# Attention and mixture of experts in one kernel: expert 0's first weights fetched later, and the slots' one-hot matmuls gathered at one place of a unit

## The chip, the cores and the metric

The kernel runs on one core of a Trainium2 chip. The metric is the device time of one execution in microseconds (us); each figure for a kernel is the median of its runs. The engines are TensorE (PE, with its weight loads PEld), VectorE (DVE), ScalarE (ACT), GpSimd (POOL) and SyncE (SP), which here only starts DMA transfers. Each engine works through its own queue in program order.

## The reference

Windowed causal attention, then a layer of 8 experts of which each token uses two:

```python
# q, k, v: [8 batches, 8 heads, 576, 64]; window 64
scores = scale * np.matmul(q, k.transpose(0, 1, 3, 2))
mask = (rel >= 0) & (rel < window)
scores = np.where(mask, scores, -1000000000.0)
...
return np.matmul(attn, v).astype(np.float32)

x = np.ascontiguousarray(attn_out.transpose(0, 2, 1, 3)).reshape(B * S, H * D)   # [4608, 512]
logits = x @ w_gate
noise_scale = np.log1p(np.exp(x @ w_noise))
noisy_logits = logits + noise_scale * noise
top2 = np.argpartition(-noisy_logits, 2, axis=1)[:, :2]
...
for e in range(E):                       # E = 8, w1[e]: [512, 1024], w2[e]: [1024, 512]
    for k in range(2):
        mask = top2[:, k] == e
        h = np.maximum(x[mask] @ w1[e], 0.0)
        out[mask] += top2_w[mask, k, None] * (h @ w2[e])
```

## The kernel before

The program has two parts. The first is a loop of 36 units (`NT`) and three more turns that empty it. A unit is one block of 64 queries of two batches (9 blocks times 4 pairs of batches), 128 tokens in all. The second part are the experts, whose matmuls take most of the time.

**The order in a unit** is written out by hand and pipelined over four units. In turn j the loop issues, in this order: the loads of k for unit j + 3; `norm_a` of unit j - 3 (VectorE, `L386` and `L387`); route steps; `scores` of j (TensorE, `L317`); the load of q for j + 3 and a piece of `w1`; `soft_a` of j and `soft_b` of j - 1 (ScalarE, a copy `L327` and the exponential `L345`); route steps; `pv` of j - 2 (TensorE, `L376`); half of `norm_b` (ScalarE, `L395`); `soft_max` and `soft_max2` of j (VectorE, the masked copy `L335` and the maximum `L340`, then GpSimd's subtraction `L341`, for which the exponential of the next turn waits); one step of the slots; `transp` of j - 1 (TensorE, `L353`); `logits` of j (TensorE, `L287`); `apply_mask` of j - 1 (VectorE, `L358`); `logits_copy` of j (ScalarE, `L293`); `gate` of j - 3 (VectorE, `L409`); one or two steps of the slots; and `aux`, the splits of expert 0's weights. `drain(rate(q))` at five places of the unit takes route steps from a list. `on(f, j)` calls f where j is a unit.

**Routing.** When the last unit of a route is gated (`ROUTE`: after units 6, 13, 20, 26 and 35), `route` adds some 45 small steps to `pending`, nearly all on VectorE and ScalarE over [128, 56] values: `L515` to `L533` turn logits into two choices for each token. `rank` counts by matmuls (`L548`, `L550`) which place each choice has in its expert's list; a yielded `HOLD` stops the list for so many calls of `drain` first. Then the `slots` steps write token numbers at these places by one-hot matmuls. For a pair of token tiles, `at_tile` makes one-hots of the high part of the place (VectorE, two `L586` for a tile), `at_lane` of the low part (two `L580` for a tile; on GpSimd while j < 36, on VectorE later), and `place` multiplies the two (four matmuls `L592` for a pair, into columns 400 and up of the bank `ps_g`, in which the logits of `L287` are too) and adds the result to `SLOT` (VectorE, `L594`). A route of seven tiles has three pairs and one single, so its lanes are 4, 4, 4 and 2 `L580`; this is called a round here. In the code before, the place matmuls of a pair are issued in the slot step that issues the next pair's lanes, wherever this falls in a unit. Names of tiles of the route all read `xc` in the profile.

**Expert 0's weights** are split into a high and a low part of a 32-bit format: eight loads of 256 KB (`load_w1`, `L214`, tile `ws`) and 16 pairs of a ScalarE copy (`L221`, tile `WH`) and a GpSimd subtraction (`L222`, tile `WL`). SyncE issues all loads and stores of the units in one queue (`qc`, `KW`, `vw`, `vt`, `xrows`).

Of the kernel before, what the change touches and what calls it, by code (L numbers as in the profile page):

```python
# [10 lines left out]
BF = mybir.dt.bfloat16  # L11
# [33 lines left out]
WARM = 4  # L45

ZFROM, ZEACH = 32, 3
HOLD = 4
RATE = ((16, 8), (99, 7))

EARLY = {14: FIRST[0], 27: FIRST[0] + FIRST[1]}
# [36 lines left out]
def tile_kernel(ctx, tc, qT, kT, vx, vT, wgx, noise, w1, w2, out):  # L88
# [363 lines left out]
    nc.vector.memset(delta, 0.0)  # L452

    def reserve(j):
        def f():
            cnt = G[:, 500:501]
            nc.tensor.matmul(cnt, lhsT=ones_b, rhs=GOT[j][:, 0, 0:1], start=True, stop=True)
            d = gw.tile([128, 57], F32, name="d0", bufs=1)[:, :1]
            nc.vector.tensor_tensor(d, cnt, delta, op=OP.add)
            nc.vector.tensor_scalar(d, d, -1.0, float(EARLY[j]), op0=OP.mult, op1=OP.add)  # L460
            nc.vector.tensor_scalar(d, d, 0.0, None, op0=OP.max)
            nc.vector.tensor_tensor(delta, delta, d, op=OP.add)
            nc.vector.tensor_tensor(ebase[:, 0:1], ebase[:, 0:1], d, op=OP.add)
        yield f
# [28 lines left out]
    def route(c):  # L493
# [9 lines left out]
        def new(name, shape=None, bufs=1):  # L503
            shape = shape or sh
            x = piece(name, [RT if d == n else d for d in shape], F32, bufs)
            return x[tuple(slice(0, d) for d in shape)]
# [34 lines left out]
                nc.vector.tensor_reduce(GOT[j1][:, 0], got.rearrange("p q e -> p e q"), op=OP.add, axis=AX.X)  # L541
        yield total
        yield HOLD
        rks = new("rks")

        def rank():
# [31 lines left out]
        def at_lane(q, x):  # L578
            for k in range(2):
                (nc.gpsimd if j < NT else nc.vector).tensor_scalar(AB[q][0][:, 2 * x + k], lane, lo[:, q + x, k:k + 1], mantissa, op0=OP.is_equal, op1=OP.mult)  # L580

        def at_tile(q, x):
            if x == 0:
                AB[q] = piece("ha", [128, 4, 128], BF, 2), piece("hb", [128, 4, E * NQ], BF, 2)
            for k in range(2):
                nc.vector.tensor_scalar(AB[q][1][:, 2 * x + k], tl.rearrange("p e q -> p (e q)"),  # L586
                                        hi[:, q + x, k:k + 1], float(1 << j0 + q + x), op0=OP.is_equal, op1=OP.mult)

        def place(q, m):
# [2 lines left out]
                nc.tensor.matmul(SP, lhsT=a[:, x], rhs=b[:, x], start=(x == 0), stop=(x == 2 * m - 1))  # L592
            v = SLOT.rearrange("p e q -> p (e q)")
            nc.vector.tensor_tensor(v, v, SP, op=OP.add)  # L594
        last = None
        for q in range(0, n, 2):
            m = min(2, n - q)
            slots.append(lambda q=q: at_tile(q, 0))
            slots.append(lambda q=q, m=m: m > 1 and at_tile(q, 1))
            slots.append(lambda q=q, m=m, f=last: (f and f(), [at_lane(q, x) for x in range(m)]))  # L600
            last = lambda q=q, m=m: place(q, m)
        slots.extend([lambda: None, lambda: None, last])

    SP = G[:, 400:400 + E * NQ]

# [16 lines left out]
        yield lambda: nc.vector.tensor_reduce(novf[:, E:E + 1], novf[:, 0:E], op=OP.add, axis=AX.X)  # L622
        yield lambda: nc.vector.tensor_copy(nov, novf)

    pending, slots = [], []


    LT, XG, XC, XH, XL, HH = {}, {}, {}, {}, {}, {}
# [17 lines left out]
    def first_list(c):  # L646
        return lists(slice(0, 1), slice(3 * c, 3 * c + len(tiles(0, c))), f"{c}")
# [123 lines left out]

    def start(c):
        def f():
            slots.append(lambda: [x() for x in first_list(c)])
            slots.append(lambda: None)
            slots.append(lambda: slots.__setitem__(slice(0, 0), gather(0, c)))
        yield f
# [227 lines left out]

    calls = [0, 0]

    def drain(n):
        calls[0] += 1
        while n and pending and calls[0] > calls[1]:  # L1010
            f = next(pending[0], None)
            if f == HOLD:
                calls[1] = calls[0] + f
            elif f:
                f()
                n -= 1
            else:
                pending.pop(0)

    def settle():  # L1020
        while pending:
            drain(10 ** 6)

    def drain_slots(n):
        while slots and n:
            slots.pop(0)()
            n -= 1
# [14 lines left out]

    aux = {}
    for q, f in enumerate(split_first(256, nc.gpsimd)):
        aux.setdefault(W1G // 2 + q // 2, []).append(f)

    def on(f, j, *a):
        if 0 <= j < NT:
# [2 lines left out]
    for j in range(NT + 3):  # L1051
        if j == TURN:
            for q, f in enumerate(turn(0, 0)):
                aux.setdefault(j + q // 2, []).append(f)

        if 0 < j < NT - 3:
            load_k(j + 3)
        on(store, j - 4)
        for _ in range(ZEACH if j >= ZFROM else 0):
            zero_out()  # L1060
        if j < 2:
            load_v(j + 2)
        if NT - 2 <= j < NT + 2:
            load_w2(0, slice((j - NT + 2) * 2, (j - NT + 3) * 2))
        on(norm_a, j - 3)
        drain(rate(0))
        on(scores, j)
        if j < NT - 3:
            load_q(j + 3)
        if W1G // 2 - 4 <= j < W1G // 2 + 4:  # L1070
            k = j - W1G // 2 + 4
            load_w1(0, slice(k // 2, k // 2 + 1), slice(k % 2 * F // 2, (k % 2 + 1) * F // 2))
        if 2 < j < 3 + len(REST):
            REST[j - 3]()
        on(soft_a, j)
        on(soft_b, j - 1)
        ahead(2)
        drain(rate(1))
        on(pv, j - 2)
        on(norm_b, j - 3, 0)  # L1080
        on(soft_max, j)
        on(soft_max2, j)
        drain_slots(1)
        if j < NP:
            warm(WARM)
        on(transp, j - 1)
        ahead(2)
        on(logits, j)
        if j < NT - 2:
            load_vt(j + 2)  # L1090
        on(norm_b, j - 3, 1)
        on(apply_mask, j - 1)
        drain(rate(2))
        on(logits_copy, j)
        ahead(2)
        on(gate, j - 3)
        drain(rate(3))
        drain_slots(4 if j >= NT else 2 if j >= DENSE else 1 + j % 2)
        for f in aux.get(j, ()):
            f()  # L1100
        drain(rate(4))
    store(NT - 1)
    for q in range(max(aux), NT + 2, -1):
        for f in aux.get(q, ()):
# [12 lines left out]
    for n, (e, c) in enumerate(work):  # L1117
        nxt = work[n + 1] if n + 1 < len(work) else None
        last = c == len(chunks(e)) - 1
        side, parts = [], []  # L1120
        if n == 0:
            halves = split_w2()
            side += halves[:5]
            parts.append((0.0, 1.0, [lambda: drain_slots(1)] * 9))

            def catch_up():
                while (0, 1, 2) not in XG:
                    drain(1)
                    drain_slots(1)
        elif n == 1:  # L1130
            pending.append(count())
            parts.append((0.0, 0.9, [lambda: (drain(1), drain_slots(1))] * 18))
            parts.append((0.0, 0.9, [zero_out] * 8))
            side += [settle, lambda: drain_slots(10 ** 6), lambda: [x() for x in first_list(2)]]
        elif c == 0:
            parts.append((0.55, 1.0, split_w2()))
        if nxt and n:
            rows_of = gather(*nxt)
            if n < 2:
                side += [lambda: None] * 2 + rows_of  # L1140
            else:
                parts.append((0.0, 0.65, rows_of))
        if last and nxt:
            nextw = split_w1(e == 0)
            parts += ([(0.55, 0.75, nextw[0]), (0.8, 1.0, nextw[1])] if e else
                      [(a, b, nextw[q]) for q, a, b in ((0, 0.02, 0.12), (1, 0.14, 0.3), (2, 0.33, 0.5), (4, 0.34, 0.5),
                                                       (3, 0.55, 0.75), (5, 0.56, 0.75), (6, 0.8, 1.0))])
        parts.append((0.92 if n == 1 else 0.0, 1.0, side))
        spread(up(e, c) if n else up00, 52 if e else KF * KD - (0 if n else len(taken)), *parts)
        side = turn(*nxt) if nxt else []  # L1150
        total = KF * len(tiles(e, c)) + (4 if e else 0)
        free = 12.5 / total
        if e == 0:
            parts = [((0.66, 0.98) if n == 0 else (0.5, 0.97) if n == 1 else (0.05, 0.85)) + (side,)]
            if last:
                parts.append((0.0, 0.4, nextw[7]))
        else:
            if c == 0:
                load_w1(e + 1)
            parts = [(free, 0.86, side)]  # L1160
            if last and nxt:
                parts.append((free, 0.9, nextw[2] + nextw[3]))
        if n == 1:
            load_w1(1)
            parts.append((0.0, 0.6, list(other_lists())))
            parts.append((0.0, 0.4, [zero_out] * len(blank)))
        if n == 0:
            parts.append((0.0, 0.16, halves[5:]))
            parts.append((0.1, 0.96, [lambda: drain(2)] * 24))
            parts.append((0.0, 0.6, [lambda: drain_slots(1)] * 6))  # L1170
            parts.append((0.64, 0.65, [catch_up]))
        spread(down(e, c), total, *parts)
        if last:
            load_w2(e + 1)
# [118 lines left out]
```

## Time and profile before

| | |
|---|---|
| time, median of 3 runs | 1024.18 us (1018.67 to 1025.19) |
| the profiled execution | 1019.5 us, its span 1017.5 us |
| mean granted TensorE clock | 0.993 of full speed |
| TensorE busy | 972.1 us, 96% of the span |
| VectorE busy | 700.9 us, 69% |
| ScalarE busy | 519.6 us, 51% |
| GpSimd busy | 319.0 us, 31% |

The span is from the first to the last recorded instruction; the profiled execution's time is some 2 us more than that. Shares are means over both parts of the program, and the units fill about the first 190 us. Where the experts begin, TensorE's share is nearly whole; in the units it is lower, and this part has to be read by stretches.

### The profile page before, as it was taken

To read this page: it belongs to the slowest core of one execution; us is meant where nothing else is said; L and a number is where in the kernel's file an instruction comes from. 1 tells how busy PE (TensorE), PEld (TensorE's weight loads), DVE (VectorE), ACT (ScalarE), POOL (GpSimd) and SP (SyncE) were. 2 spreads that over 40 slices of the span, in tenths; PEclk is the share of its full clock that TensorE was granted. 3 is DMA by queue.
4 is the path that set the end of the run, shared out by engine and by line. 5 is a ranking of instruction groups with operands and counts; after the bars stand their busy time and mean duration, and the time that the engine had idled before them with its cause. 6 is when DMAs were issued, how large, how long until landed. Compare 5 with 4: busy or idle time off the path is not lost.

```text
span 1017.5 us, 22099 instructions
## 1 busy us (share of the span) xinstructions
PE 972.1 (96%) x8464; PEld 869.0 (85%) x8464; DVE 700.9 (69%) x1830; ACT 519.6 (51%) x1310; POOL 319.0 (31%) x436
## 2 busy tenths in 40 slices
PE   8788887899999999999999999999999999999995
PEld 8777776788889898989898989898989899889994
DVE  5698899665686668666866685777677766776630
ACT  4887676531445445544554454445454554455430
POOL 4446555121412323231313241414140414042202
PEclk9999999999999999999999999999999999999998
DMA  9989889647567553765485548655854585466303
GB/s 332 366 277 299 262 271 345 203 103 249 127 157 171 121 144 64 220 140 140 79 234 110 140 90 212 139 123 108 242 95 117 122 242 96 104 142 152 47 2 53
DMA packets 107235, 168.94 MB, mean 166 GB/s; under 512 B 13360, under 2 KB 57648, under 8 KB 105328
## 3 DMA queue, kind: packets, MB, share of 16 engines
q1 hardware_dynamic: 89968, 126.96, 41.1%
q0 software_dynamic: 17152, 40.48, 22.6%
q8 instruction: 68, 1.11, 0.5%
q14 instruction: 47, 0.39, 0.1%
HBM read 110.08 MB, written 57.32 MB: 165 GB/s over the span
## 4 chain that ended last, share of the span: by engine, by line
PE 80%; DVE 7%; DMA 4%; ACT 4%; issue 2%; POOL 1%; SPq 0%; POOLq 0%; DVEq 0%; ACTq 0%
PE ps_d L987 8%; PE ps_d L985 8%; PE ps_d L986 8%; PE ps_z L841 6%; PE ps_z L843 6%; PE ps_z L842 6%; DMA vt<-in_vT_dram 3%; PE ps_v L841 3%; PE ps_v L842 3%; PE ps_v L843 3%; PE ps_y L987 2%; PE ps_y L986 2%; PE ps_y L985 2%; PE ps_y L842 2%; PE ps_y L843 2%
## 5 line engine op out<-in xcount | busy, mean ns | idle before, releaser
L919 POOL DMA_INDIRECT out_dram<-xg,los x70 | 110.1, 1573 | 397.0 <-ACT xg L998 364.5
L987 PE MATMUL ps_d<-w2h,hb 128*128 128x512 f32 x392 | 153.2, 391 | 0.0
L985 PE MATMUL ps_d<-w2h,hb 128*128 128x512 f32 x392 | 153.2, 391 | 0.0
L986 PE MATMUL ps_d<-w2l,hb 128*128 128x512 f32 x392 | 152.8, 390 | 0.0
L853 ACT ACTIVATE hb<-tq 128x288 fp32r<-128x288 f32 (+1 forms) x168 | 77.1, 459 | 144.0 <-DVE tq L872 143.9
L872 DVE TENSOR_TENSOR tq<-ps_z,tq 128x288 f32<-128x288 f32 (+1 forms) x168 | 79.3, 472 | 88.0 <-PE ps_z L843 87.1
L841 PE MATMUL ps_z<-xh,WH 128*128 128x288 f32 (+1 forms) x448 | 137.2, 306 | 0.9
L843 PE MATMUL ps_z<-xh,WL 128*128 128x288 f32 (+1 forms) x448 | 135.0, 301 | 0.0
L842 PE MATMUL ps_z<-xl,WH 128*128 128x288 f32 (+1 forms) x448 | 135.0, 301 | 0.0
L857 DVE SCALAR_TENSOR_TENSOR hb<-tq,hb 128x320 fp32r<-128x320 f32 (+2 forms) x168 | 75.6, 450 | 37.5 <-ACT hb L853 35.3
L660 POOL DMA_INDIRECT xg<-xrows,lxs x70 | 70.0, 1000 | 87.5 <-DMA xs<-xg 35.7
L841 PEld LDWEIGHTS ps_z<-xh,WH 128*128 128x128 f32 x448 | 84.0, 188 | 5.6 <-DVE tq L872 3.8
L987 PEld LDWEIGHTS ps_d<-w2h,hb 128*128 128x128 f32 x392 | 73.6, 188 | 16.0
L986 PEld LDWEIGHTS ps_d<-w2l,hb 128*128 128x128 f32 x392 | 73.6, 188 | 14.1
L985 PEld LDWEIGHTS ps_d<-w2h,hb 128*128 128x128 f32 x392 | 73.6, 188 | 14.1
L842 PEld LDWEIGHTS ps_z<-xl,WH 128*128 128x128 f32 x448 | 84.1, 188 | 1.3
L843 PEld LDWEIGHTS ps_z<-xh,WL 128*128 128x128 f32 x448 | 84.1, 188 | 0.0
L234 DVE TENSOR_TENSOR WL<-ws,WH 128x512 fp32r<-128x512 f32 x112 | 67.1, 614 | 6.5 <-ACT WH L242 6.5
L395 ACT ACTIVATE x<-ps_o,r 128x80 f32<-128x80 f32 x288 | 66.7, 346 | 8.8 <-DVE r L387 8.5
L744 ACT ACTIVATE xh<-tq 128x512 fp32r<-128x512 f32 (+1 forms) x70 | 42.7, 610 | 51.9 <-DVE tq L740 49.7
L724 DVE STREAM_TRANSPOSE tq<-xc 128x256 f32<-128x256 f32 (+1 forms) x140 | 52.0, 409 | 15.2 <-DMA xc<-xs 13.9
L341 POOL TENSOR_TENSOR t<-t,mx 128x512 f32<-128x512 f32 x36 | 37.9, 1052 | 77.9 <-DVE mx L340 60.5
(238 smaller groups left out, 2392.7 us busy)
## 6 DMA issues: line engine op xcount, KB each, us to landing
ws<-in_w_dram SPq DMA_DIRECT2D x14, 2048.0 KB, 11.6
xs<-xg SPq DMA_DIRECT2D x63, 256.0 KB, 3.6
vw<-in_vx_dram SPq DMA_DIRECT2D x36, 272.0 KB, 5.0
out_dram<-zero SPq DMA_DIRECT2D x38, 256.0 KB, 5.6
qc<-in_qT_dram SPq DMA_DIRECT2D x36, 256.0 KB, 5.1
KW<-in_kT_dram SPq DMA_DIRECT2D x36, 256.0 KB, 4.6
vt<-in_vT_dram SPq DMA_DIRECT2D x36, 256.0 KB, 4.4
xrows<-x SPq DMA_DIRECT2D x36, 256.0 KB, 4.7
```

Of the source, the lines that this page charges most:

```text
L234: eng.tensor_tensor(l, x, h.bitcast(F32), op=OP.subtract)
L660: nc.gpsimd.indirect_dma_start(out=XG[e, c, q][:m], out_offset=None, in_=X[:DUMP + seen.get((e, c), NT) * 128], in_offset=bass.IndirectOff ...
L841: nc.tensor.matmul(p[:, :n], lhsT=WH[:, a, k, w], rhs=xh[:, b, k, :n], start=first and k == 0, stop=False, **free)
L842: nc.tensor.matmul(p[:, :n], lhsT=WH[:, a, k, w], rhs=xl[:, b, k, :n], start=False, stop=False, **free)
L843: nc.tensor.matmul(p[:, :n], lhsT=WL[:, a, k, w], rhs=xh[:, b, k, :n], start=False, stop=(k == 1), **free)
L853: nc.scalar.activation(hh[:, f, a:b], src, AF.Relu)
L857: nc.vector.scalar_tensor_tensor(hl[:, f, a:m], src[:, :m - a], 0.0, hh[:, f, a:m].bitcast(F32), op0=OP.max, op1=OP.subtract)
L872: nc.vector.tensor_tensor(t, a[:, :n], t, op=OP.add)
L919: s = nc.gpsimd.indirect_dma_start(out=out[:(2 + seen.get((e, c), NT)) * 128], out_offset=bass.IndirectOffsetOnAxis(ap=LT[e, c][1][q][:m], ...
L985: nc.tensor.matmul(p, lhsT=h, rhs=w2h[:, f, :], **a)
L986: nc.tensor.matmul(p, lhsT=h, rhs=w2l[:, f, :], start=False, stop=False)
L987: nc.tensor.matmul(p, lhsT=l, rhs=w2h[:, f, :], **b)
```

## The change

Two things move, and some small ones go with them.

The loads and splits of expert 0's first weights: the eight `load_w1` pieces are issued in units 12, 14, ..., 26 in place of units 2 to 9, and the 16 splits one in each of the units 15 to 30 in place of two in each of the units 6 to 13.

The place step: a pair's `place` is put in a list `owed` with the turn's number, and issued by `placing` right after `scores`, one turn later; in the tail (from turn 39 on) by `drain_slots`, three calls later. The one-hots get a third buffer. Steps of a route that use TensorE (`rank`, `reserve`) yield a mark `PE` and are only taken at the drain that stands between `scores` and `pv`. `HOLD` is 3 and no longer 4. Before the token lists are first read (`first_list`), what is owed is issued. Line numbers of the changed kernel are one to six higher here: `L317` becomes `L318`, `L340` `L341`, `L341` `L342`, `L592` `L598`, `L594` `L600`, `L580` `L584`.

```diff
-HOLD = 4
+HOLD = 3
+PE = "pe"
...
     def reserve(j):
+        yield PE
+
...
         yield HOLD
+        yield PE
         rks = new("rks")
...
             if x == 0:
-                AB[q] = piece("ha", [128, 4, 128], BF, 2), piece("hb", [128, 4, E * NQ], BF, 2)
+                while len(owed) > 2:
+                    owed.pop(0)[1]()
+                AB[q] = piece("ha", [128, 4, 128], BF, 3), piece("hb", [128, 4, E * NQ], BF, 3)
...
-        last = None
         for q in range(0, n, 2):
...
-            slots.append(lambda q=q, m=m, f=last: (f and f(), [at_lane(q, x) for x in range(m)]))
-            last = lambda q=q, m=m: place(q, m)
-        slots.extend([lambda: None, lambda: None, last])
+            slots.append(lambda q=q, m=m: ([at_lane(q, x) for x in range(m)],
+                                           owed.append((clock[0], lambda: place(q, m)))))
...
-            slots.append(lambda: [x() for x in first_list(c)])
+            slots.extend([lambda: None] * 3 + [lambda: (flush(), [x() for x in first_list(c)])])
...
-    def drain(n):
+    kept = []
+
+    def drain(n, pe=True):
...
-            f = next(pending[0], None)
+            f = kept.pop() if kept else next(pending[0], None)
...
+            elif f == PE:
+                if not pe:
+                    kept.append(f)
+                    return
...
+    def placing(lag):
+        clock[0] += 1
+        if owed and clock[0] - owed[0][0] >= lag:
+            owed.pop(0)[1]()
+
+    def flush():
+        while owed:
+            owed.pop(0)[1]()
+
     def drain_slots(n):
+        if clock[0] >= NT + 3:
+            placing(3)
...
-        aux.setdefault(W1G // 2 + q // 2, []).append(f)
+        aux.setdefault(W1G + 3 + q, []).append(f)
...
-        drain(rate(0))
+        drain(rate(0), False)
         on(scores, j)
+        placing(1)
         if j < NT - 3:
             load_q(j + 3)
-        if W1G // 2 - 4 <= j < W1G // 2 + 4:
-            k = j - W1G // 2 + 4
+        if W1G <= j < W1G + 16 and j % 2 == 0:
+            k = (j - W1G) // 2
             load_w1(0, slice(k // 2, k // 2 + 1), slice(k % 2 * F // 2, (k % 2 + 1) * F // 2))
...
-        drain(rate(2))
+        drain(rate(2), False)
...
-        drain(rate(3))
+        drain(rate(3), False)
...
-        drain(rate(4))
+        drain(rate(4), False)
```

In the rows of the two programs' order, a row is a line, its operation, and output and inputs by name with a size; a count at the end joins equal rows. TensorE in the first round, before: the last place matmul of a pair, then the rest of that unit (transposes, logits), then the next unit's scores and pv.

```order
L592 LDWEIGHTS xc
L592 MATMUL ps_g<-xc 128x80
L353 MATMUL ps_t<-ident,p 128x128 x4
L287 MATMUL ps_g<-wgx_sb,vt 128x64 x4
L317 MATMUL ps_s<-KW,qc 64x128 x16
L376 MATMUL ps_o<-vw_91,pt 64x85 x32
```

And in the changed program, at the same pv:

```order
L598 LDWEIGHTS xc
L598 MATMUL ps_g<-xc 128x80
L377 MATMUL ps_o<-vw_91,pt 64x85 x32
L354 MATMUL ps_t<-ident,p 128x128 x4
L288 MATMUL ps_g<-wgx_sb,vt 128x64 x4
L318 MATMUL ps_s<-KW,qc 64x128 x16
```

The place matmuls moved from between pv and the transposes to between scores and pv.

VectorE at the same place, before: a route step, the masked copy and the maximum of the unit, the addition to `SLOT`, the mask.

```order
L520 TENSOR_TENSOR xc<-xc,noise_sb 128x56
L522 TENSOR_TENSOR xc<-lg,xc 128x56
L335 COPY_PREDICATED t<-mprev,ps_s 128x512
L340 TENSOR_REDUCE mx<-t 128x8
L594 TENSOR_TENSOR SLOT<-SLOT,ps_g 128x80
L358 TENSOR_TENSOR pt<-ps_t,maskT 128x1024
L527 TENSOR_REDUCE xc<-xc 128x7
```

And changed:

```order
L523 TENSOR_TENSOR xc<-xc,noise_sb 128x56
L600 TENSOR_TENSOR SLOT<-SLOT,ps_g 128x80
L525 TENSOR_TENSOR xc<-lg,xc 128x56
L336 COPY_PREDICATED t<-mprev,ps_s 128x512
L341 TENSOR_REDUCE mx<-t 128x8
L359 TENSOR_TENSOR pt<-ps_t,maskT 128x1024
L530 TENSOR_REDUCE xc<-xc 128x7
```

The addition now stands ahead of the masked copy and the maximum.

SyncE's queue in units 2 and 3, before: loads of q, of expert 0's weights (`ws`), of v in two layouts and of k.

```order
L117 DMA qc<-in_qT_dram 128x512
L214 DMA ws<-in_w_dram 128x512
L130 DMA vw_90<-in_vx_dram 128x544
L136 DMA vt<-in_vT_dram 128x512
L121 DMA KW<-in_kT_dram 128x512
```

And changed:

```order
L118 DMA qc<-in_qT_dram 128x512
L131 DMA vw_90<-in_vx_dram 128x544
L137 DMA vt<-in_vT_dram 128x512
L122 DMA KW<-in_kT_dram 128x512
L118 DMA qc<-in_qT_dram 128x512
```

The piece of weights has left the queue, which is otherwise in the same order.

## Rows read from the trace of the kernel before

**Rows 1.** Busy by stretch: length, PE, PEld, DVE, ACT, POOL, clock, DMA share, GB/s.

```profile
35.50:47.00 11.50, 8.27 (x218) 7.33 (x216) 6.66 (x13) 8.41 (x30) 5.73 (x7) 1.00 1.01 374
47.00:67.60 20.60, 15.65 (x441) 14.18 (x440) 17.88 (x45) 18.15 (x65) 9.86 (x12) 1.00 0.94 308
...
115.00:135.00 20.00, 15.73 (x444) 14.23 (x437) 18.57 (x62) 13.91 (x54) 15.54 (x18) 1.00 0.88 288
...
206.00:1017.00 811.00, 798.35 (x4457) 713.06 (x4455) 538.08 (x1363) 380.99 (x819) 222.58 (x303) 1.00 0.58 134
```

**Rows 2.** DMA view, 0 to 60 us: packets, MB, share; an issue.

```profile
q1 hardware_dynamic: 11511, 20.41, 96.6%
...
ws<-in_w_dram SPq DMA_DIRECT2D x8, 256.0 KB, 5.6
```

**Rows 3.** TensorE's timeline, units 4 to 14: start, length, work, idle before.

```profile
19.98 1.10 PE L317 MATMUL ps_s<-KW,qc 64*64 64x128 f32 x32
...
35.55 1.10 PE L317 MATMUL ps_s<-KW,qc 64*64 64x128 f32 x32
...
38.02 0.81 PE L376 MATMUL ps_o<-vw,pt 64*64 64x85 f32 x29 [0.65 <-issue]
...
45.16 0.51 PE L376 MATMUL ps_o<-vw,pt 64*64 64x85 f32 x11 [2.42 <-issue]
...
67.63 1.10 PE L317 MATMUL ps_s<-KW,qc 64*64 64x128 f32 x32
```

**Rows 4.** Timeline of all engines around one split, at 53 us.

```profile
52.98 0.72 ACT L221 ACTIVATE WH<-ws 128x256 fp32r<-128x256 f32 x2
...
53.47 1.44 POOL L222 TENSOR_TENSOR WL<-ws,WH 128x256 fp32r<-128x256 f32 x2 [0.57 <-ACT WH L221]
53.66 0.63 DVE L520 TENSOR_TENSOR xc<-xc,noise_sb 128x56 f32<-128x56 f32 x1
```

**Rows 5.** Timeline of all engines, units 17 and 18.

```profile
84.52 1.04 POOL L341 TENSOR_TENSOR t<-t,mx 128x512 f32<-128x512 f32 x1 [3.45 <-DVE SLOT L594]
...
85.54 3.31 POOL L580 TENSOR_SCALAR xc<-lane,xc,mantissa 128x128 bf16<-128x128 bf16 x4
...
87.62 0.18 DVE L520 TENSOR_TENSOR xc<-xc,noise_sb 128x56 f32<-128x56 f32 x1
...
87.97 0.72 DVE L335 COPY_PREDICATED t<-mprev,ps_s 128x512 f32<-128x512 uint32 x1
...
88.72 0.69 DVE L340 TENSOR_REDUCE mx<-t 128x8 f32<-128x512 f32 x1
...
88.91 0.21 PE L592 MATMUL ps_g<-xc 128*128 128x80 bf16 x1 [0.56 <-POOL xc L580]
...
89.32 0.23 DVE L594 TENSOR_TENSOR SLOT<-SLOT,ps_g 128x80 f32<-128x80 f32 x1
89.56 1.04 POOL L341 TENSOR_TENSOR t<-t,mx 128x512 f32<-128x512 f32 x1 [0.70 <-DVE SLOT L594]
```

**Rows 6.** GpSimd's timeline: the `L341` that begin and end rounds.

```profile
104.93 1.04 POOL L341 TENSOR_TENSOR t<-t,mx 128x512 f32<-128x512 f32 x1 [4.91 <-DVE mx L340]
...
115.27 1.10 POOL L341 TENSOR_TENSOR t<-t,mx 128x512 f32<-128x512 f32 x1 [3.57 <-DVE mx L340]
...
135.12 1.04 POOL L341 TENSOR_TENSOR t<-t,mx 128x512 f32<-128x512 f32 x1 [1.95 <-DVE mx L340]
...
150.26 1.05 POOL L341 TENSOR_TENSOR t<-t,mx 128x512 f32<-128x512 f32 x1
...
172.51 1.04 POOL L341 TENSOR_TENSOR t<-t,mx 128x512 f32<-128x512 f32 x1 [2.79 <-DVE mx L340]
```

**Rows 7.** TensorE's waits in the place step: us in total, times, longest.

```profile
PE ps_g L592 <- ACT vw L293: 6.9, 10, 0.9
...
PE ps_g L592 <- DVE xc L580: 2.4, 2, 1.4
```

**Rows 8.** Busy time, 100 to 105 us, with the granted clock.

```profile
100.00:105.00 5.00, 4.12 (x102) 3.57 (x105) 2.40 (x7) 2.37 (x9) 0.09 (x2) 0.74 0.78 222
```

More of the change, by code (lines that the diff above doesn't have):

```diff
@@ L623, in count @@
         yield lambda: nc.vector.tensor_copy(nov, novf)
-    pending, slots = [], []
+    pending, slots, owed, clock = [], [], [], [0]
     LT, XG, XC, XH, XL, HH = {}, {}, {}, {}, {}, {}
@@ L1133, in tile_kernel @@
             parts.append((0.0, 0.9, [zero_out] * 8))
-            side += [settle, lambda: drain_slots(10 ** 6), lambda: [x() for x in first_list(2)]]
+            side += [settle, lambda: (drain_slots(10 ** 6), flush()), lambda: [x() for x in first_list(2)]]
         elif c == 0:
```

## The prediction

> **What bounds the kernel now.** I read busy time by stretch first. From 206 us on, TensorE is busy for 798.35 of 811.00 us [rows 1]: the experts' matmuls run back to back, and the change touches none of them. So the change is decided in the units, before 206 us, and a microsecond saved or lost there is one at the end. There I read three stretches. From 35.5 to 47 us TensorE is busy for 8.27 of 11.50 us and the DMA engines are full (1.01); from 47 to 67.6 us VectorE is busy for 17.88 of 20.60; from 115 to 135 us for 18.57 of 20.00 [rows 1]. The early units are short of something else than TensorE, and the later ones, with the one-hots in them, of VectorE. Then the DMA view of the first 60 us: the queue that SyncE starts fills 96.6% of sixteen engines, and eight `ws` loads of 256 KB (2.1 of 20.41 MB) are in it [rows 2]. TensorE's timeline gives the pace: units 4 to 7 go from 19.98 to 35.55 us, 3.89 each; units 8 to 13 from 35.55 to 67.63, 32.1 us for six [rows 3].
>
> **Part 1, what leaves the early units.** Eight loads leave units 2 to 9, and the 16 splits leave units 6 to 13. Six units at 32.1 us stand against 3.89 each. I read the gaps as two kinds. In units 8 and 9 TensorE stands for 0.65 and 2.42 us inside the pv matmuls with "issue" as the reason, while the DMA engines are full [rows 1, 3]; with a tenth fewer bytes queued I let these two units fall to 3.9. In units 10 to 13 VectorE is the bound: 17.88 us for four units, 4.47 each. Part of that is stretch: `L520` takes 0.63 us beside `L222` [rows 4], and 0.18 where GpSimd runs `L580` [rows 5]; six VectorE operations of these units stand like that (the others 0.42 to 0.67 in place of about 0.2), some 2.3 us. Without it VectorE needs (17.88 - 2.3) / 4 = 3.9; I take 4.3, between that and 4.47, since waits remain. So 2 x 3.9 + 4 x 4.3 = 25.0, and the term is **-7.1 us**. The ends: all six at 3.89 would give -8.8; only the stretch and one small gap going (2.3 + 0.65), -3.
>
> [...]
>
> **Part 2, the place matmuls.** Before, the four `L592` of a pair stand half a unit or more behind the scores; now they stand right behind scores and ahead of pv, and their VectorE addition stands ahead of the copy `L335` and the maximum `L340` of the same unit. The operands are the same: four `L580` on GpSimd, which start only after the previous unit's `L341`. That closes a ring. Unit 17 shows every link [rows 5]: `L341` at 84.52, the four `L580` from 85.54 for 3.31, ending at 88.85; the fourth matmul waits for them (0.56) and the addition ends at 89.55, 0.70 later. Before, `L335` (87.97) and `L340` (88.72) had run by then, and the next `L341` began at 89.56. Now they come after the addition: 0.75 from `L335` to `L340`, 0.84 from `L340` to `L341`. The ring is 1.02 + 3.31 + 0.70 + 0.75 + 0.84 = **6.6 us** for each unit with four `L580`, and 6.6 - 1.65 = 5.0 for one with two. VectorE's other work (mask, gate, route steps, `L586`) fits beside the 3.31 us; TensorE's pv, transposes and logits queue behind the waiting `L592`, but need less than the ring leaves.
>
> A route's round has three units with four and one with two: 3 x 6.6 + 5.0 = 24.8 us. There are three while GpSimd does the lanes. Now, by the `L341` at their ends, they take 104.93 - 84.52 = 20.4, 135.12 - 115.27 = 19.9 and 172.51 - 150.26 = 22.3 [rows 5, 6]. The term is 4.4 + 4.9 + 2.5 = **+11.9 us**. The removed waits of `L592` for the logits copy (`L293`, 6.9 us, ten times) [rows 7] lie mostly inside these rounds, so they are already in the 20.4, 19.9 and 22.3 and bring nothing beside them. Ends: +8, if a unit with two `L580` keeps the pace of 4.3 and each ring is 0.2 shorter; +15, if a further VectorE operation of 0.2 or 0.3 stands in each of the twelve rings.
>
> **Part 3, loads and splits in units 12 to 30.** 2.1 MB more go through the units 12 to 26, some 70 us long; from 115 to 135 us the DMA share is 0.88, not full [rows 1]. Each split is 0.72 us of GpSimd (two in 1.44) and 0.36 of ScalarE [rows 4]. In the ring GpSimd stands idle for 0.70 + 0.75 + 0.84 = 2.3 us per unit, so `L222` fits. Outside the rounds GpSimd is mostly idle. What is not free is the neighbour: a VectorE operation with two SBUF operands lost 0.45 us (0.63 against 0.18) beside `L222`. Nine of the splits fall into rounds, where this could lie in the ring: at most 9 x 0.45 = +4. Below zero nothing speaks for it, since no work goes. I take **+0.5**, as the chain's own operations (`L335`, `L340`, the addition) each have at most one large SBUF operand and the bulk of the splits meets no two-input step.
>
> [...]
>
> **Part 4, the tail.** From unit 36 on, the one-hots come from VectorE, and TensorE waited 2.4 us for `L580` in two places [rows 7]. Placing three calls later removes them: **-2.4** (0 if the chain behind is late anyway, -4 if the clock's fall after them goes too). Buffers, the pieces that wait for the scores, and the hold of three in place of four shift route steps by a unit at most; I cost them at nothing, covered by the units' own spare time, and their failure is inside the ends above.
>
> **The sum.** -7.1 + 11.9 + 0.5 - 2.4 = +2.9. The profiled run took 1019.5 us, 4.7 under the median of 1024.18, and would take 1022.4; on the median's footing the forecast is **1027 us**. With all ends together it is -4.8 to +16 (-8.8 + 8 + 0 - 4; -3 + 15 + 4 + 0), 1019 to 1040.
>
> **The rivals.** First, *the ring does not close*: the matmuls find their lanes ready. Then -7.1 - 2.4 and some 3 us of the 6.9 of removed waits give 1024.2 - 12.5 = 1012. For it: the waits on `L293` are real. Against it: in unit 17 the last matmul, half a unit later than it now stands, still waited 0.56 us for them [rows 5]. Chance 0.15.
>
> Second, on the other side, *the clock falls in the rounds*. TensorE was busy for 15.73 of 20.00 us in the second round [rows 1] and would be for about 4.1 of 6.6, less of its time than in any stretch shown at 1.00. [...] Chance 0.14.
>
> [...] Chance 0.13, and 0.58 for the forecast.
>
> **How the numbers follow.** Under 1% either way this kernel's measurement tells nothing from no change: 1014 to 1034.4. Faster: nearly all of the first rival's 0.15, 0.14. Slower: the second's 0.14, half of the third, and 0.03 of the forecast's upper end, 0.23. Same: 0.63. The range of 8 in 10 leaves out the second rival and about half of the first: 1013 to 1040.
>
> **What would show it.** In the profile after: matmuls of the place step waiting for GpSimd's lanes about nine times, around 2 us each; the `L341` 6.6 us apart in the rounds; no wait for the logits copy; the scores of unit 14 at about 60.5 in place of 67.63; no stretched `L520` before that; the tail's two waits gone. The prediction is wrong if rounds keep 20 us (first rival), if the clock in them falls well under 1.00 for whole units (second), or if unit 14 starts after 64 us (third).

## The result, and the profile after

Measured beside each other, the changed kernel took 1032.12 us (median of 7 runs, 1029.5 to 1035.91) and the kernel before 1022.69 (7 runs); the ratio is 1.0102, with a 95% interval of 1.0073 to 1.013. So it is 1% slower. The forecast was 1027 on a median of 1024.18, 0.3% slower, with a range of 1013 to 1040.

The profiled execution took 1031.57 us, its span 1029.7, 12.2 over the span before, at a mean granted clock of 0.982 (0.993 before). GpSimd's timeline of the changed kernel shows the subtractions `L342` that begin the units in the rounds (answering to [rows 5, 6]); a row with `L342` is start, length, work, idle before and its releaser.

```profile
81.86 1.04 POOL L342 TENSOR_TENSOR t<-t,mx 128x512 f32<-128x512 f32 x1 [2.08 <-DVE mx L341]
...
88.62 1.04 POOL L342 TENSOR_TENSOR t<-t,mx 128x512 f32<-128x512 f32 x1 [1.59 <-DVE mx L341]
...
95.36 1.10 POOL L342 TENSOR_TENSOR t<-t,mx 128x512 f32<-128x512 f32 x1 [1.87 <-DVE mx L341]
...
101.73 1.04 POOL L342 TENSOR_TENSOR t<-t,mx 128x512 f32<-128x512 f32 x1 [1.45 <-DVE mx L341]
...
108.64 1.04 POOL L342 TENSOR_TENSOR t<-t,mx 128x512 f32<-128x512 f32 x1 [2.92 <-DVE mx L341]
...
119.08 1.10 POOL L342 TENSOR_TENSOR t<-t,mx 128x512 f32<-128x512 f32 x1 [2.80 <-DVE mx L341]
...
143.75 1.04 POOL L342 TENSOR_TENSOR t<-t,mx 128x512 f32<-128x512 f32 x1 [1.46 <-DVE mx L341]
...
159.94 1.05 POOL L342 TENSOR_TENSOR t<-t,mx 128x512 f32<-128x512 f32 x1
...
185.24 1.04 POOL L342 TENSOR_TENSOR t<-t,mx 128x512 f32<-128x512 f32 x1 [2.81 <-DVE mx L341]
```

The first four stand 6.76, 6.74 and 6.37 us apart, as the ring asked; the fourth unit, with two lanes, takes 6.91 in place of 5.0. TensorE's timeline of that unit, with its lanes, shows why:

```profile
102.76 1.56 POOL L584 TENSOR_SCALAR xc<-lane,xc,mantissa 128x128 bf16<-128x128 bf16 x2
...
103.81 1.99 PE L318 MATMUL ps_s<-KW,qc 64*64 64x128 f32 x32
```

The two lanes end at 104.32 us, but the scores, at 1.99 us in place of 1.10, only at about 105.7, and the place matmuls, behind both, start at 105.73. The granted clock is 0.56 over this unit, so here the low clock sets the pace and not the lanes. The rounds take 26.78, 24.67 and 25.30 us, by the rows' differences; before 20.41, 19.85 and 22.25.

The timeline of all engines of the changed kernel shows the ring's first turn (answering to [rows 5]).

```profile
82.15 1.10 PE L318 MATMUL ps_s<-KW,qc 64*64 64x128 f32 x32
...
82.88 3.45 POOL L584 TENSOR_SCALAR xc<-lane,xc,mantissa 128x128 bf16<-128x128 bf16 x4
...
86.39 0.21 PE L598 MATMUL ps_g<-xc 128*128 128x80 bf16 x1 [0.56 <-POOL xc L584]
...
86.53 1.81 PE L377 MATMUL ps_o<-vw,pt 64*64 64x85 f32 x64
86.71 0.24 DVE L600 TENSOR_TENSOR SLOT<-SLOT,ps_g 128x80 f32<-128x80 f32 x1 [1.81 <-ACT x L396]
...
87.03 0.73 DVE L336 COPY_PREDICATED t<-mprev,ps_s 128x512 f32<-128x512 uint32 x1
87.79 0.69 DVE L341 TENSOR_REDUCE mx<-t 128x8 f32<-128x512 f32 x1
```

The four lanes `L584` begin behind `L342` of 81.86. Scores (82.15) are long done; each of the four place matmuls waits for its lane, the last for 0.56 us; only then does the addition `L600` run, and behind it `L336` and `L341`, and the next `L342` begins at 88.62. Pv (`L377`) starts at 86.53, though the scores end at 83.25.

TensorE's timeline of the changed kernel has the scores that open units 8, 10 and 14 and the two gaps inside pv (answering to [rows 3]); its waits in the place step answer to [rows 7]: us in total, times, longest.

```profile
35.36 1.10 PE L318 MATMUL ps_s<-KW,qc 64*64 64x128 f32 x32
...
38.60 0.81 PE L377 MATMUL ps_o<-vw,pt 64*64 64x85 f32 x29 [1.41 <-issue]
...
43.13 0.51 PE L377 MATMUL ps_o<-vw,pt 64*64 64x85 f32 x11 [0.25 <-issue]
...
45.00 1.10 PE L318 MATMUL ps_s<-KW,qc 64*64 64x128 f32 x32
...
62.42 1.10 PE L318 MATMUL ps_s<-KW,qc 64*64 64x128 f32 x32
```

```profile
PE ps_g L598 <- POOL xc L584: 13.6, 20, 2.5
...
PE ps_g L598 <- DVE xc L584: 2.0, 1, 2.0
...
PE ps_g L598 <- DVE SLOT L600: 1.3, 1, 1.3
```

Unit 14 begins at 62.42 us (67.63 before). The wait for the logits copy is gone, and 13.6 us of waits for GpSimd's lanes are in its place, against 6.9. The tail still waits, once for 2.0 us on VectorE's lanes and once for 1.3 on `SLOT`.

Busy time by stretch in the three rounds (columns as in [rows 1]: PE, PEld, DVE, ACT, POOL, then granted clock, DMA share, GB/s):

```profile
81.90:108.60 26.70, 22.23 (x445) 19.19 (x444) 18.96 (x58) 15.94 (x56) 18.24 (x22) 0.74 0.75 242
119.10:143.80 24.70, 18.50 (x421) 15.72 (x413) 18.59 (x61) 15.91 (x57) 18.60 (x23) 0.86 0.76 246
160.00:185.20 25.20, 19.34 (x419) 16.66 (x420) 19.38 (x62) 14.28 (x49) 16.06 (x19) 0.86 0.85 291
```

VectorE, 18.57 of 20.00 us in the second round before, now does the same work in 24.70, and the clock is 0.74, 0.86 and 0.86. It falls unevenly: in the first round it is 0.91, 0.59, 0.94 and 0.56 over the four units.

Added up along the run, after against before: unit 14 starts 5.2 us earlier; from there to the first round 2.6 of that are lost (19.44 against 16.89 us); the rounds lose 6.4, 4.8 and 3.1; the stretches between them lose 0.1 and 1.1 (10.44 and 16.19 us against 10.34 and 15.14); from the last round to the end 0.5 is gained. The sum is 12.2. These are two single executions; the medians differ by 9.4.

### The profile page after: what moved, and what is told of

It is laid out like the page before. It is cut to its first block, busy times and chain, and to the rows that moved or that the text cites. A ratio compares the mean times of both kernels' runs of the same rounds, so it can differ in the third digit from the quotient of the medians.

```text
span 1029.7 us, 22104 instructions
## 1 busy us (share of the span) xinstructions
PE 981.0 (95%) x8464; PEld 877.3 (85%) x8464; DVE 701.0 (68%) x1830; ACT 521.6 (51%) x1310; POOL 319.9 (31%) x436
## 4 chain that ended last, share of the span: by engine, by line
PE 82%; DVE 8%; POOL 3%; issue 3%; ACT 2%; DMA 1%; SPq 0%; POOLq 0%; DVEq 0%; ACTq 0%
PE ps_d L991 8%; PE ps_d L989 8%; PE ps_d L990 8%; PE ps_z L845 6%; PE ps_z L847 6%; PE ps_z L846 6%; PE ps_o L377 3%; PE ps_v L845 3%; PE ps_y L990 2%; PE ps_y L991 2%; PE ps_y L989 2%; PE ps_v L847 2%; PE ps_v L846 2%; POOL xc L584 2%; PE ps_y L846 2%
## 5 line engine op out<-in xcount | busy, mean ns | idle before, releaser
L342 POOL TENSOR_TENSOR t<-t,mx 128x512 f32<-128x512 f32 x36 | 38.0, 1056 | 86.8 <-DVE mx L341 83.6
```

## The experiments

Twelve kernels ran. Times are ratios to the kernel before, run beside them on the same chip. Rounds are the first, second and third, from the `L341` (or `L342`) that begin and end them.

| kernel | ratio, 95% interval | rounds, us |
|---|---|---|
| before | 1 | 20.4, 19.9, 22.3 |
| changed | 1.0102 (1.0073 to 1.013) | 26.8, 24.7, 25.3 |
| loads and splits only | 0.9995 (0.997 to 1.0019) | 19.6, 20.2, 22.1 |
| place step only | 1.0119 (1.0082 to 1.0156) | 25.9, 25.6, 24.9 |
| changed, addition late | 1.0106 (1.0071 to 1.0141) | 26.2, 25.7, 27.0 |
| changed, place late | 1.0023 (0.9998 to 1.0049) | 21.7, 24.0, 24.7 |
| splits only | 1.0 (0.9969 to 1.0031) | 20.2, 21.2, 21.5 |
| changed, TensorE kept busy | 1.0165 (1.0131 to 1.0199) | 26.6, 26.9, 33.8 |
| addition late, kept busy | 1.0164 (1.0123 to 1.0205) | 25.7, 24.0, 31.8 |
| place late, kept busy | 1.0029 (1.0006 to 1.0052) | 25.2, 24.0, 25.1 |
| changed, half of the lanes on VectorE | 1.0032 (1.0013 to 1.005) | 24.2, 23.0, 25.5 |
| changed, two turns | 0.9968 (0.9945 to 0.9991) | 19.9, 21.0, 23.4 |
| two turns, half of the lanes | 0.999 (0.9972 to 1.0007) | 22.5, 21.6, 24.8 |
| before, half of the lanes | 1.003 (1.0004 to 1.0056) | 21.2, 22.7, 26.0 |

**The two parts apart.** The first kernel is the one before with the loads and splits moved:

```diff
-        aux.setdefault(W1G // 2 + q // 2, []).append(f)
+        aux.setdefault(W1G + 3 + q, []).append(f)
...
-        if W1G // 2 - 4 <= j < W1G // 2 + 4:
-            k = j - W1G // 2 + 4
+        if W1G <= j < W1G + 16 and j % 2 == 0:
+            k = (j - W1G) // 2
```

> Only the loads and splits move; the place step is as before. Theory (the two parts add up, and the loss is the ring's): unit 14 starts near 62 us as in the changed kernel, the units 14 to 17 lose some 2.5 us of that to the loads there, the rounds stay near 20.4, 19.9 and 22.3 us with at most 0.7 more for a unit with a split in it; in all within 4 us of before, 1019 to 1026 on the median's footing. Rival (the splits in the rounds are what costs, by the neighbour on VectorE): rounds 2 us longer each or more, time 1027 or more.

It measured 0.9995, with unit 14 at 64.03 us and the rounds as the theory had them. The second is the changed kernel with these lines put back, so that the place step alone is moved.

> Only the place step (with its buffers, marks and hold) moves; loads and splits are as before. Theory (ring): the L341 of a round stand 6.4 to 6.9 us apart although no split is near, rounds of 25 to 27 us, unit 14 at about 67.6, so 12 to 15 us over before, 1035 to 1039. Rival (the rounds are long because the splits stand in them): rounds near 20 to 22 us, within 4 us of before.

It measured 1.0119. Its `L342`, with no split anywhere near:

```profile
86.20 1.04 POOL L342 TENSOR_TENSOR t<-t,mx 128x512 f32<-128x512 f32 x1 [4.71 <-DVE mx L341]
...
92.94 1.04 POOL L342 TENSOR_TENSOR t<-t,mx 128x512 f32<-128x512 f32 x1 [2.26 <-DVE mx L341]
...
99.39 1.09 POOL L342 TENSOR_TENSOR t<-t,mx 128x512 f32<-128x512 f32 x1 [2.27 <-ACT x L396]
...
105.85 1.04 POOL L342 TENSOR_TENSOR t<-t,mx 128x512 f32<-128x512 f32 x1 [2.14 <-DVE mx L341]
...
112.08 1.04 POOL L342 TENSOR_TENSOR t<-t,mx 128x512 f32<-128x512 f32 x1 [3.63 <-DVE mx L341]
```

They are 6.74, 6.45, 6.46 and 6.23 us apart. So the whole loss is the place step's (with its marks and hold, which the kernel with two turns below keeps), it needs no split, and the loads and splits together are worth nothing that can be measured.

**Where the ring closes.** In the next kernel only VectorE's addition moves, behind the maximum:

```diff
             for x in range(2 * m):
                 nc.tensor.matmul(SP, lhsT=a[:, x], rhs=b[:, x], start=(x == 0), stop=(x == 2 * m - 1))
-            v = SLOT.rearrange("p e q -> p (e q)")
-            nc.vector.tensor_tensor(v, v, SP, op=OP.add)
+            def add():
+                v = SLOT.rearrange("p e q -> p (e q)")
+                nc.vector.tensor_tensor(v, v, SP, op=OP.add)
+            adds.append(add)
...
+    def adding():
+        while adds:
+            adds.pop(0)()
...
         on(soft_max2, j)
+        adding()
```

> The changed kernel with one VectorE operation moved: the addition to SLOT goes behind the masked copy and the maximum of the unit. TensorE's order is untouched, so its matmuls still wait for the lanes ahead of pv. Theory (the ring closes on VectorE): units with four lanes fall from 6.4 to 6.9 to 5.1 to 5.4 us, rounds 20 to 22, time 9 to 12 us under the changed kernel, 1020 to 1024. Rival (it closes on TensorE, pv queued behind the waiting matmuls): rounds stay at 24 us or more, time within 4 us of the changed kernel.

It measured 1.0106, so the rival came out: opening the ring on VectorE alone brings nothing. Its timeline shows why.

```profile
83.01 1.04 POOL L342 TENSOR_TENSOR t<-t,mx 128x512 f32<-128x512 f32 x1 [2.06 <-DVE mx L341]
...
87.61 0.21 PE L598 MATMUL ps_g<-xc 128*128 128x80 bf16 x1 [0.57 <-POOL xc L584]
...
87.74 2.55 PE L377 MATMUL ps_o<-vw,pt 64*64 64x85 f32 x64
...
88.20 1.04 POOL L342 TENSOR_TENSOR t<-t,mx 128x512 f32<-128x512 f32 x1
...
93.37 1.41 PE L377 MATMUL ps_o<-vw,pt 64*64 64x85 f32 x64
...
96.75 1.07 POOL L342 TENSOR_TENSOR t<-t,mx 128x512 f32<-128x512 f32 x1 [2.75 <-DVE SLOT L602]
...
97.81 3.12 POOL L584 TENSOR_SCALAR xc<-lane,xc,mantissa 128x128 bf16<-128x128 bf16 x4
...
101.17 2.54 PE L377 MATMUL ps_o<-vw,pt 64*64 64x85 f32 x64
```

The first unit is indeed short: `L342` at 88.20, 5.19 us after that of 83.01. But pv is behind the waiting matmuls and starts at 87.74, then runs at the low clock (0.50 from 88 to 90 us; 2.55 us for 64 matmuls that take 1.41 in the next unit, at 93.37, with the clock at 1.00); the next scores start at 92.09, and through the copy, `L336`, `L341`, `L342` (96.75) and its lanes (97.81 to 100.93) the next pv starts at 101.17. From pv to pv these are 101.17 - 87.74 = 13.43 us for two units, 6.7 each: a second ring, which passes through TensorE and is as long as the one through VectorE alone. Not all of its length is order: pv at the low clock has 1.1 us of it. The edit also adds a wait of its own: the logits, which go into the same bank `ps_g` as the place matmuls, now wait for the late addition, 3.3 us in five waits.

Moving the matmuls behind pv as well opens that one too:

```diff
         on(scores, j)
-        placing(1)
...
         on(soft_max2, j)
+        placing(1)
```

> The changed kernel with the whole place step moved: matmuls behind pv, addition behind the maximum. Theory (the ring closes on VectorE alone): as with the addition alone, within 2 us of it, since pv has slack behind the lanes. Rival (both engines hold it): 3 us or more under the kernel with only the addition moved, 1016 to 1019.

It measured 1.0023: 8 of the 10 us are back, so both engines hold it, as the rival said, though not all of the time that it gave. The largest wait in the place step that is left is that of the logits for the addition, which use the same bank, 6.1 us in seven waits; how much of the remaining time it makes is not shown. Among TensorE's waits in this kernel it is:

```profile
PE ps_g L288 <- DVE SLOT L600: 6.1, 7, 1.8
```

**The distance in turns.** This kernel leaves the place step ahead of pv and of the masked copy, where the change put it, and only issues it two turns after its lanes:

```diff
-        placing(1)
+        placing(2)
```

> The changed kernel with the place step two turns after its lanes in place of one, at the same place in the unit; TensorE's and VectorE's order is else unchanged. Theory (the ring is closed by the one-turn distance between lanes and place): no matmul of the place step waits for the lanes, the clock stays near 1.00 in the rounds, rounds of 19.5 to 22.5 us, time at the level of before, 1018 to 1025. Rival (place ahead of pv and of the masked copy costs by itself): rounds of 24 us or more, 1028 or more.

It measured 0.9968, at or a little under before, and no wait for the lanes is among TensorE's longer ones; its rounds run at a clock of 1.00, 1.00 and 0.93, by stretch:

```profile
82.60:102.50 19.90, 17.04 (x449) 14.50 (x448) 18.79 (x57) 15.84 (x57) 18.18 (x23) 1.00 0.91 300
112.60:133.60 21.00, 17.90 (x465) 15.57 (x468) 19.30 (x60) 16.05 (x59) 18.32 (x23) 1.00 0.89 304
149.30:172.60 23.30, 20.11 (x481) 18.08 (x479) 20.35 (x63) 15.00 (x53) 16.50 (x20) 0.93 0.97 315
```

So the place in the unit costs nothing by itself; the one turn between lanes and place does. It is the fastest of all, though its rounds are not shorter than before's (64.2 us against 62.5 in all, the third a little longer than expected) and its profile does not show where 0.3% comes from.

**The length of the lanes.** Half of a pair's lanes go to VectorE:

```diff
-                (nc.gpsimd if j < NT else nc.vector).tensor_scalar(...)
+                (nc.gpsimd if j < NT and not x else nc.vector).tensor_scalar(...)
```

> The changed kernel with half of the lanes of a pair on VectorE (some 0.25 us each there, from the tail) and half on GpSimd (1.65 us in place of 3.31). Theory (whatever engine closes the ring, the lanes are its longest link): units of 6.4 to 6.9 us fall by about 1.5 to 5.0 to 5.4, rounds to 20 to 22, time 8 to 13 us under the changed kernel, 1020 to 1025. Rival (the low clock behind TensorE's waits sets the pace): rounds of 23.5 us or more, time within 5 us of the changed kernel.

It measured 1.0032, 0.7% or 7 us under the changed kernel, a little short of the 8 to 13 expected, and its rounds (24.2, 23.0, 25.5) are between the two expectations. VectorE is the full engine now: it is busy for 16.4 of the 16.7 us from 81.79 to 98.47. Its timeline shows where some of that comes from: two of its lanes need 0.54 us, or 1.32 where GpSimd's `L342` runs.

```profile
88.04 1.32 DVE L584 TENSOR_SCALAR xc<-lane,xc,mantissa 128x128 bf16<-128x128 bf16 x2
...
88.26 1.04 POOL L342 TENSOR_TENSOR t<-t,mx 128x512 f32<-128x512 f32 x1 [2.79 <-DVE mx L341]
...
96.68 0.54 DVE L584 TENSOR_SCALAR xc<-lane,xc,mantissa 128x128 bf16<-128x128 bf16 x2
```

The same edit on top of the two turns, and on the kernel before:

> Two turns and half of the lanes on VectorE. Theory (once the ring is open the lanes lie beside other work, and VectorE, with 0.5 us more a unit, is the fuller engine): 0 to 4 us over the kernel with two turns alone. Rival (GpSimd's cycle of subtraction, four lanes and a split, some 5.1 us, is the next bound): 3 to 6 us under it, and under before.

> The kernel before with half of the lanes on VectorE, nothing else. Theory (in its rounds VectorE is the bound, at 18.57 of 20 us): rounds 0 to 2 us longer each, time 0 to 5 us over before. Rival (GpSimd's 1.04 + 3.31 us with a wait of 0.7 bounds its units at 5.04): rounds 1 to 2 us shorter each, time 3 to 6 us under before, and the best version of all.

They measured 0.999 against the 0.9968 without it, and 1.003: with the ring open or absent VectorE is the fuller engine (18.79 us of 19.90 in the first round with two turns, GpSimd 18.18), and GpSimd's lanes are better left where they are. In both cases the theory held for the time; two rounds of the second grew by 2.8 and 3.7 us, more than it said.

**The clock.** Ten matmuls of ones stand ahead of the place matmuls (six in the third kernel), into columns that nobody reads:

```diff
+            for _ in range(10 if clock[0] <= NT else 0):
+                nc.tensor.matmul(idle[:, 336:400], lhsT=ones, rhs=ones[:, 0:64], start=True, stop=True)
             owed.pop(0)[1]()
```

> The changed kernel with ten matmuls of ones (some 2.5 us) between scores and the place matmuls in the units that place, whose results nobody reads; they only keep TensorE busy while it would wait for the lanes. Theory (in the changed kernel the ring through VectorE sets the pace of units with four lanes, the clock adds little): the clock in the rounds rises towards 1.00, the L341 stay 6.4 to 6.8 us apart with four lanes and fall to about 5.0 with two; 2 to 4 us under the changed kernel, 1028 to 1031. Rival (the low clock makes the rounds long): units fall to 5 to 5.5 us, time 1022 or less.

In the first round, at a granted clock of 1.00, `L342` come at 81.89, 88.67, 95.09 and 101.55; the first row is TensorE's, the other two are busy time by stretch:

```profile
86.43 0.21 PE L598 MATMUL ps_g<-xc 128*128 128x80 bf16 x1 [0.56 <-POOL xc L584]
```

```profile
82.00:101.60 19.60, 18.97 (x394) 17.39 (x392) 14.32 (x50) 12.35 (x43) 15.00 (x19) 1.00 0.77 254
168.00:180.00 12.00, 12.00 (x135) 11.25 (x134) 5.42 (x20) 3.40 (x12) 5.26 (x6) 0.50 0.58 184
```

That is 6.78, 6.42 and 6.46 us with four lanes at full clock, and the links follow each other as before: `L342` at 88.67, the lanes from 89.70 to 92.85, the addition at 93.22, `L336` at 93.49, `L341` at 94.26, the next `L342` at 95.09. So the low clock of the changed kernel goes with the ring and does not make it, with one reserve: TensorE, with the added matmuls, was nearly full too (18.97 of 19.60). The first unit is free of that reserve: its last place matmul, at 86.43, still waited 0.56 us for its lane, and the unit took 6.78. The unit with two lanes is no test: it took 6.90 in place of the 5.0 expected, as the added matmuls alone run there from 103.39 to 105.83, behind the end of the lanes (104.14). The time got longer nevertheless (1.0165), which neither expected: in the third round a gap still came (TensorE was busy for 0.58 us from 164 to 166), the clock fell to 0.50 between 168 and 180 us, and the added matmuls, ten in 4.53 us there and in 2.44 at a clock of 1.00, made units of 10.9 and 9.0 us.

> The kernel with the addition behind the maximum, and the same ten matmuls. Theory (with the ring through VectorE opened, what held the rounds at 26 us was TensorE, idle before the lanes and then at the low clock behind them): units of 5.2 to 5.6 us, rounds of 20 to 22, time 9 to 13 us under the kernel without the ten matmuls, 1021 to 1025. Rival (the bank shared by place and logits, whose matmuls then wait for the addition, holds the units at any clock): rounds of 24 us or more, time within 5 us of it.

> The kernel with the whole place step behind pv and maximum, and six of these matmuls between pv and the place matmuls. Theory (clock): rounds from 21.7, 24.0 and 24.7 us to 20 to 22, time 3 to 6 us under that kernel, 1019 to 1022, at or under before. Rival (the shared bank): rounds as they were, time within 2 us or longer by the matmuls.

These two are no test. With the addition late TensorE was busy for 25.64 of 27.00 us from 82 us on, because without them it had been idle for less than they take (4.65 us of 26.20 in the first round, against some 2.44 for the ten of each unit), so these set the pace themselves (1.0164); with the place late the ratio stayed at 1.0029 against 1.0023, as its rival had it, but the clock was not lifted in all rounds either (0.86, 0.93 and 0.93, against 0.93, 0.83 and 0.89 without the matmuls, over somewhat longer stretches from 83, 114 and 155 us). How much of the 26 us in the rounds of the kernel with the late addition is the clock's stays open.

**The early units.** Only the splits move, the loads stay in units 2 to 9:

```diff
-        aux.setdefault(W1G // 2 + q // 2, []).append(f)
+        aux.setdefault(W1G + 3 + q, []).append(f)
```

> The kernel before with only the splits moved; the loads stay in units 2 to 9. Theory (the early gain is both VectorE's neighbour and the loads; the loss in units 14 to 17 is the moved loads): unit 14 starts between the 64 of the kernel with loads and splits moved and the 67.6 of before, and the units 14 to 17 take some 17 us as in before, not 19. [...] Time within 4 us of before either way.

The expectation does not fit. Unit 14 starts at 68.30, so all of the early gain is gone: it needs the loads to leave. And units 14 to 17 are as long as with the loads moved (from the `L341` of unit 13 at 66.82 to that of unit 17 at 87.28 it takes 20.5 us; before 18.35, in the changed kernel 19.9): the loss there does not need the loads. The timeline of one of these units:

```profile
76.17 0.42 DVE L586 TENSOR_SCALAR xc<-tl,xc 128x80 bf16<-128x80 f32 x2
...
76.39 1.10 POOL L341 TENSOR_TENSOR t<-t,mx 128x512 f32<-128x512 f32 x1 [3.49 <-DVE mx L340]
...
77.47 3.17 POOL L580 TENSOR_SCALAR xc<-lane,xc,mantissa 128x128 bf16<-128x128 bf16 x4
...
80.52 1.87 DVE L586 TENSOR_SCALAR xc<-tl,xc 128x80 bf16<-128x80 f32 x2
...
80.62 0.72 POOL L222 TENSOR_TENSOR WL<-ws,WH 128x256 fp32r<-128x256 f32 x1
...
81.30 1.04 POOL L341 TENSOR_TENSOR t<-t,mx 128x512 f32<-128x512 f32 x1
```

GpSimd has the subtraction, four lanes and the split in one row: 1.10, 3.17 and 0.72 us bring the next `L341` to 81.30, 4.91 us after the last; in the kernel before this unit took 4.22 (75.81 to 80.03). Beside the split and the subtraction that follows it, two `L586` of VectorE take 1.87 us, in place of 0.42 at 76.17. The other part is a gap of 1.40 us inside pv with "issue" as its reason. In units 14 to 16 these gaps sum to 0.8 us in the kernel before, 2.4 here, 2.1 with loads and splits moved and 2.8 in the changed kernel. The run with the place step alone, whose loads and splits are where they were before, has them too, 2.4 us in two gaps:

```profile
74.55 0.96 PE L377 MATMUL ps_o<-vw,pt 64*64 64x85 f32 x37 [0.96 <-issue]
...
80.24 0.65 PE L377 MATMUL ps_o<-vw,pt 64*64 64x85 f32 x18 [1.40 <-issue]
```

There the way from the scores of unit 14 (67.53) to the `L342` of unit 17 (86.20) takes 18.7 us, against 16.9 before and 19.4 in the changed kernel. So most of the loss in these units needs neither the loads nor the splits. The kernel before with half of the lanes on VectorE has 0.8 us of gaps again. Why they grow in every kernel with any of the three moves is not settled by any run.

## Why the prediction came out as it did

*What bounds the kernel, and where the change is decided*: right. From the last round to the end the kernels differ by 0.5 us.

*Part 1* (-7.1): it measured -5.2 at unit 14, inside its ends. Units 10 to 13 took 17.42 us, 4.36 each, as the 4.3 taken. Units 8 and 9 are the term that was off: 9.64 us in place of 7.8, since gaps of 1.41 and 0.25 us with "issue" stay in pv although the loads had left. That the loads' leaving closes them even in part is not shown: they are 1.66 us here against 3.07, but 2.99 in the run with loads and splits moved, and 1.5 in the run with the place step alone, where the loads stay. What makes these gaps no row shows. In units 10 to 13 one reading was off: four of the six stretched operations stand there (0.50 to 0.67 us, some 1.6 of stretch in place of 2.3), and the other two, at 67.94 and 68.83 us, already in unit 14. With only the splits away these four units took 18.9 us against 20.6 before, which is about this stretch; the 17.4 of the changed kernel came with both moves, and with only the splits away units 8 and 9 took 2 us more.

*Part 2* (+11.9): the ring stands in the trace as worked out, 6.4 to 6.9 us against 6.6, and the rounds lost 14.2. The missing 2.3 are mostly the first round's unit with two lanes, 6.91 against 5.0, at a granted clock of 0.56, where the scores at the low clock ended 1.4 us behind the lanes. One thing in the comparison was not said: in the kernel before the first round's first four lanes ran two units earlier, at 76.89, so its 20.41 us hold lanes of 4, 4, 2 and none, while the changed kernel has 4, 4, 4 and 2 in these units. One step was incomplete: the prediction let the ring close by the addition ahead of the copy and the maximum, and held that pv, transposes and logits "need less than the ring leaves". The run with the addition late shows a second ring through just these, 6.7 us a unit, with the low clock in it. With the first ring opened the time stayed where it was (1.0106), so the second, with the low clock and the wait that the edit adds, suffices for the loss; what both share, and what two turns undo, is the one turn between lanes and place.

*Part 3* (+0.5): 3.7 us stand against it, but they are not shown to be the loads' and the splits'. From unit 14 to the first round 2.6 us were lost and between the second and third 1.1, and the run with the splits alone has the first of these. The term had looked for the cost inside the rounds, where loads and splits alone added nothing (61.9 us in all against 62.5); 2 us of the 2.6 are longer "issue" gaps in pv (2.8 against 0.8), which no term had counted. The run with the place step alone loses 1.8 of the 2.6 with gaps of 2.4, so the cost came with any of the moves, and its cause stays open. Where a unit with lanes comes before the round, as in the run with the splits alone, the split also stands ahead of the next subtraction in GpSimd's own queue (0.7). The term's reason, that the chain's own operations have at most one large SBUF operand, is half borne out. In the changed kernel they kept their length: `L336` took 0.69 to 0.76 us, `L341` 0.69 and `L600` 0.19 to 0.24. But one such operand does not make an operation safe beside GpSimd: in the run with half of the lanes on VectorE two lanes, with one 128x128 tile as input, took 1.32 us in place of 0.54 and ended at 89.36, `L342` at 89.30. What decides which operations stretch was not shown.

*Part 4* (-2.4): failed. The later placing did not remove the waits: from the last round to the end 0.5 us were gained; one wait of 2.0 us and one of 1.3 stand where two of 0.97 and 1.44 stood.

*The rivals.* The first did not occur: the lanes are not ready. The second occurred in part: the clock fell to 0.74 and 0.86 in the rounds, and to 0.59 and 0.56 over two whole units. The ring hid most of that: the unit at 0.59, with four lanes, took 6.74 us, beside 6.76 and 6.37 for its neighbours at 0.91 and 0.94; the one at 0.56, with two lanes, took 6.91 in place of 5.0. What a clock that is low throughout the rounds would cost, on which 0.14 of the chance of a slower kernel stands, no run shows. The third did not occur: unit 14 came at 62.42 and not after 64. The total of +2.9 stands against 12.2 in the profiled executions (9.4 in the medians), and is off by four terms of one sign: 1.9, 2.3, 3.2 and 1.9. No errors cancelled. The time still lies in the range because each part stayed within its own ends, and the range was built from all of them; the forecast in its middle was a third of what was lost, or less.

## What to carry to other kernels

A step that consumes another engine's work and is put at an earlier place of a loop may need one more turn of distance: with one turn everything queued behind it on its own engine, and behind what depends on it, joined a ring with the producer here (1.0102), and with two it did not (0.9968). Work out the ring's length from one unit of the trace, all links, and look for a second ring on the other engine before hoping to open the first. And charge a loss to a moved piece only when the run without that move does not have the loss: here the place step alone lost most of what stood beside the moved loads and splits.

## What the hardware showed

In the run with half of the lanes on VectorE, two of its one-hot operations (`L584`, one 128x128 tile as input) that started at 88.04 us, beside GpSimd's subtraction of 88.26, took 1.32 us and ended at 89.36, 0.06 after it; at 96.68, beside GpSimd's two lanes of 95.61 and no subtraction, two took 0.54. With ten matmuls of ones ahead of the place matmuls the granted clock was 1.00 in the first round (0.74 without them), and the third took 33.8 us against 25.3 in the changed kernel, with the clock at 0.50 from 168 to 180 us. Gaps with "issue" in pv over units 14 to 16 sum to between 1.7 and 3.6 us in twelve kernels, with 54 or 55, 37 or 18 of a unit's 64 matmuls still to come; in the two kernels that keep the loads, the splits and the place step where they were they sum to 0.8, and stand ahead of all 64.
